# Fused window attention and FFN on one Trainium2 core: from head 12 on, the score products of attention in plain float32 on 64x32 tiles instead of split float32r operands

## Chip, core and metric

The kernel runs on one core of a Trainium2 chip. The metric is device time in microseconds (us), the median of repeated runs. TensorE (PE) does all matrix products. VectorE (DVE), ScalarE (ACT) and GpSimd (POOL) do the elementwise work. SyncE (SP) issues nearly all DMAs.

## The reference

Eight batches of eight heads (64 heads), 512 local and 32 global rows of 64 floats for each head. Every global query sees all 544 keys. A local query sees the 32 global keys and the local keys at most 32 positions away. The rows of all heads then go through a two-layer FFN. Cut to what matters:

```python
k_all = np.concatenate([k_g, k_l], axis=2)
s_g = scale * np.matmul(q_g, k_all.transpose(0, 1, 3, 2))
out_g = np.matmul(sm(s_g), v_all)                 # sm: softmax, sum + 1e-9
s_ll = scale * np.matmul(q_l, k_l.transpose(0, 1, 3, 2))
s_ll = np.where(np.abs(pos[:, None] - pos[None, :]) <= 32, s_ll, -1e9)
s_lg = scale * np.matmul(q_l, k_g.transpose(0, 1, 3, 2))
out_l = np.matmul(sm(np.concatenate([s_lg, s_ll], -1)), np.concatenate([v_g, v_l], 2))
x = concat([out_g, out_l]).transpose(0, 2, 1, 3).reshape(4352, 512)
h = x @ w_in; y = (h - np.tanh(h)) @ w_out        # w_in 512x2048, w_out 2048x512
```

## The kernel before, in words

**FFN.** Each batch's 512 local rows are one chunk, and the 256 global rows are a last one. A chunk has 16 steps. A step is 12 matmuls into the hidden layer (L1062; L1088 for the first chunk's first steps) and 12 out of it (L1125). Operands are float32 numbers split into a rounded high part and a rest, both float32r, and each product is three passes (high x high, high x rest, rest x high). After each step ACT takes tanh (L1070), DVE subtracts (L1073), and the result is split again (L346, L1079).

**Attention, heads 0 to 11** ("plain"). Keys and queries are float32, two heads at a time (a pair) on partitions 0 to 63 and 64 to 127. A float32 product of two plain operands leaves two matmul records in the trace for each matmul in the program. Local scores (L643) are 64-row tiles, 224 columns for each block of 128 queries. Global scores (L553, L554) are 512 and 96 columns for both heads of a pair. Probabilities are transposed by TensorE (L1019) into `turned`, and the products with the values (L695) take both heads side by side, each on 64 columns of the array: 18 + 19 blocks of 32 columns, 1184 columns for each head.

**Attention, heads 12 to 63.** Each head's keys and queries are loaded (L741), transposed by DVE in 32x32 blocks (L745), rounded to a high part and a rest (L346, L754), and moved from partitions to partitions by SP's DMAs, so that high and rest lie on top of each other: keys into `kw` (L843, four DMAs a head), queries within `hi` and `hl` (L848, two a head). Then a head's local scores are eight matmuls of 224 columns with 128 rows (L929 rest, L930 high), and its global scores are two (L878, L879; 384 and 224 columns). DVE takes the maximum (L934, L890), ACT the exponential (L941, L896), POOL the division (L953, L905). Heads 12 to 15 still transpose on TensorE (L1019, two visits of four matmuls a head). From head 16 on (`MOVE`) DVE transposes 32x32 blocks (L997), a DMA writes them to DRAM (`moved`, L1001), and seven DMAs a pair bring them back into `turned` (L675). Global probabilities go over `gt` (L980, then L346).

**What sets the order.** Everything is given to a list scheduler (`Order`) as an operation with an engine, an estimated time, a due time (from the table `CFG`), and the keys it reads and writes. `run()` simulates the engines and writes the instructions in the order of its simulated starts, one fixed order for each engine. On the chip each engine follows its order and waits on semaphores. Attention of a batch is laid between the FFN steps of the batch before. `turned`, the probability buffers and the loaded raw keys and queries have one copy each, and attention uses the PSUM banks 0 to 2.

Of the kernel before, what the change touches and what calls it, by code (L numbers as in the profile page):

```python
# [32 lines left out]
class Later:  # L33


    def __init__(self, pool, shape, tag):
        self.make = lambda: pool.tile(shape, F32R, name=tag, tag=tag)
        self.tile = None
# [167 lines left out]
def kernel(ctx, tc, q_l, k_l, v_l, q_g, k_g, v_g, w_in, w_out, out):  # L206
# [12 lines left out]
    dr = ctx.enter_context(tc.tile_pool(name="dr", bufs=1, space=bass.MemoryType.DRAM))  # L219
# [3 lines left out]
    MOVE = 16  # L223
    PLAIN = 6
    stats_all = cp.tile([P, 4, 16], F32, name="stats")
    stats = [stats_all[:, j] for j in range(4)]
    gt = cp.tile([P, 5, G], F32, name="gt")
# [5 lines left out]
    raw1, kq = rawkq[:, :S], rawkq[:, S:]  # L233
    wraw01 = cp.tile([P, 512, 2], F32, name="wraw01")
    wraw2 = cp.tile([P, 512], F32, name="wraw2")
# [8 lines left out]
    vraw = cp.tile([P, 2, NT, D], F32, name="vraw")  # L244
    joined = [vraw.rearrange("p a t d -> p (a t d)"), wraw2]
# [26 lines left out]
    moved = [dr.tile([P, KC // 32, 2 * NT, 32], F32, name=f"moved{j}") for j in range(2)]  # L272
# [5 lines left out]
    prob = [cp.tile([P, 2 * KC + G], F32, name=f"prob{j}") for j in range(2)]  # L278
# [8 lines left out]
    kw2 = Later(cp, [P, NT, KC], "kw")  # L287
    hi0, hl = Later(cp, [P, S], "hi0"), Later(cp, [P, 2, S], "hl")

    def parts_hi(u):  # L290
        return hl()[:, 0] if u else hi0()

    def part_lo():
        return hl()[:, 1]
# [4 lines left out]
    kgt = Later(cp, [P, H * G], "kgt")  # L299
    qgt = Later(cp, [P, H, 2, G], "qgt")  # L300
# [10 lines left out]
    def bank(shape, j, dt=F32):  # L311
# [6 lines left out]
        elif len(shape) == 4:  # L318
# [4 lines left out]
    CFG = dict(a_g=0.0823, a_gl=20.3051, a_kg=5.3644, a_kq=1.7694, a_ph=9.8391, a_qs=37.5681, a_w=0.3044, a_wn=43.1857, a_xg=33.2801, d_g=63.4309,  # L323
               d_gl=20.8802, d_kg=0.5854, d_kq=14.1069, d_ph=0.45, d_qh=26.732, d_qs=0.6609, d_tg=1.5033, d_tp=30.9704, d_w=35.4231, d_wl=106.2853,
               d_wn=0.9146, d_xg=67.7167, d_y=44.1556, gfirst=0, ho=563.7252, hs=263.6934, lag=-554.6717, last=0.0, newb=2, o_ld=-6186.7772,
               o_pv=-1166.4422, o_pvp=715.1637, o_s=-1347.6614, o_sg=-1415.5434, o_sp=-135.3597, o_t=241.5756, o_tg=456.811, o_tn=-6827.0521,
               o_tpp=-435.6543, o_rd=921.0591, o_vl=-3274.0645, p0=59.5136, pen=45.3181, penp=-188.1742, s_g=44.266, s_gl=16.9975, s_kq=26.1855,
               s_ql=65.9933, s_w=66.4348, s_wl=19.1856, step=539.4635, step1=134.0641, lag0=-705.3437, hs0=198.8445, tol=0.01097, wd0=-392.1115,
               wsp=62.3079, xw=7.7743182, o_ld0=208.6561, o_tn0=444.0832, o_sg0=755.2869, o_tg0=-488.1267, o_s0=-1015.1146, o_sp0=-1339.9745,
               o_t0=786.6386, o_tpp0=12.6795, o_vl0=5.0533, o_vl1=-1566.8932, o_pv0=1125.121, o_pvp0=1054.5986, o_ld1=1734.2237, o_pv1=248.4066,  # L330
               o_pvp1=443.4492, o_s1=-272.1136, o_sg1=-1114.1941, o_sp1=1078.4169, o_t1=339.8555, o_tg1=-620.4031, o_tn1=-475.6504, o_tpp1=659.0213,
               wsp1=13.077, ho0=1146.9578, mw=0.0683195, o_h0=1295.0637, hp=-258.3577, bp0=395.8109, bp1=-328.4325, bp2=-95.9109, bp3=-555.0465,
# [147 lines left out]
    class Pair:  # L480
# [170 lines left out]
        def add_norms(self, p):  # L651
# [11 lines left out]
            for norm, due, st, x in n:  # L663
                add(("P", 0.89), norm, due, r=[st], w=[x])

        def add_fetch(self):
            src = moved[self.j % 2]
            mv = [("mv", self.j % 2, h, p) for h in range(2) for p in range(2)]

# [61 lines left out]

    def add_transposed(name, n, loads, due, u, xfer):

        def load(e, _):
# [659 lines left out]
```

## Time and profile before

| what | value |
|---|---|
| runs, median (lowest to highest) | 975.27 us (974.46 to 976.32) |
| profiled execution, span on the page | 979.0 us (no other time of it is given) |
| TensorE busy, share | 945.6 us, 97% |
| VectorE, ScalarE, GpSimd busy | 601.2, 506.0, 452.1 us |
| granted TensorE clock, mean | 0.992 |
| DMA moved | 129.23 MB; 48.8% of the 16 engines' span for SP's queue |
| last products with the values begin | 828.4 us |

The profiled span is 3.7 us (0.4%) above the median. "Busy" counts an engine while an instruction runs. TensorE's matmuls overlap, so the time one costs is the distance from its start to the next start, not its own length.

### The profile page before, as it was taken

The page shows a single profiled execution, that of the slowest core. Times are in us where ns is not written, and L with a number is a line of the kernel's source. Part 1 is how long each engine was busy: PE and PEld are TensorE (multiplying, and loading weights), DVE is VectorE, ACT ScalarE, POOL GpSimd, SP SyncE. Part 2 cuts the span into 40 slices and gives each one's busy share as a digit, 9 for nine tenths or more (in the row PEclk, how much of TensorE's full clock was granted, in tenths as well). Part 3 has the DMA queues.
Part 4 walks back from the last instruction along what each step waited for, and adds up shares of the span by engine and source line. Part 5 has one row for each costly group of instructions (what it writes and reads, how often), then busy time and mean ns, then how long its engine had stood idle before and what let it go on. Part 6 is the DMA issues. An engine that isn't in the chain of part 4 may idle for free.

```text
span 979.0 us, 17478 instructions
## 1 busy us (share of the span) xinstructions
PE 945.6 (97%) x5246; PEld 774.5 (79%) x5246; DVE 601.2 (61%) x2116; ACT 506.0 (52%) x1381; POOL 452.1 (46%) x560
## 2 busy tenths in 40 slices
PE   7899999999999999999999999999999999999998
PEld 5676787787888788878788778887788788888897
DVE  6876578777747784678738774678738775111110
ACT  5875676755536554555537554565537543222221
POOL 4565767554535453454435553454436442222221
PEclk8999999999999999999999999999999999999999
DMA  8556466577766676677656775677657772100000
GB/s 212 157 137 157 145 174 170 135 162 158 166 137 162 155 161 144 140 162 173 139 113 167 158 167 121 140 163 171 137 114 170 161 179 61 44 1 1 14 31 22
DMA packets 363103, 129.23 MB, mean 132 GB/s; under 512 B 301952, under 2 KB 349952, under 8 KB 363008
## 3 DMA queue, kind: packets, MB, share of 16 engines
q1 hardware_dynamic: 301680, 112.08, 48.8%
q10 hardware_dynamic: 61328, 16.03, 7.1%
q8 instruction: 42, 0.69, 0.3%
q14 instruction: 53, 0.43, 0.2%
HBM read 61.98 MB, written 30.93 MB: 95 GB/s over the span
## 4 chain that ended last, share of the span: by engine, by line
PE 69%; DMA 9%; DVE 7%; ACT 5%; SPq 4%; issue 2%; POOL 2%; ACTq 0%; DVEq 0%; POOLq 0%
PE bank L1125 28%; PE bank L1062 28%; PE bank L695 5%; DMA hl<-hl 3%; PE bank L929 2%; ACT prob L941 2%; SPq L741 2%; PE bank L930 2%; DMA moved<-wraw 1%; POOL prob L953 1%; DVE prob L934 1%; DVE t L1073 1%; DMA out_dram<-wraw 1%; DMA first_q<-in_moe_w_in_dram 1%; SPq L848 1%
## 5 line engine op out<-in xcount | busy, mean ns | idle before, releaser
L1079 POOL TENSOR_TENSOR gates<-t,gates 128x512 fp32r<-128x512 f32 x136 | 176.8, 1300 | 287.0 <-PE bank L1125 181.6
L1125 PE MATMUL bank<-w_out_hi,gates 128*128 128x512 f32 x1088 | 297.0, 393 | 3.1 <-ACT gates L346 2.3
L1125 PEld LDWEIGHTS bank<-w_out_hi,gates 128*128 128x128 f32 x1088 | 202.0, 188 | 47.1 <-ACT gates L346 2.9
L1073 DVE TENSOR_TENSOR t<-bank,t 128x512 f32<-128x512 f32 x136 | 93.5, 688 | 183.9 <-ACT t L1070 182.6
L1070 ACT ACTIVATE t<-bank 128x512 f32<-128x512 f32 x136 | 81.1, 597 | 170.1 <-PE bank L1062 156.8
L1125 PE MATMUL bank<-w_out_lo,gates 128*128 128x512 f32 x544 | 151.9, 393 | 0.1
L1062 PE MATMUL bank<-x_hi,w_in_lo 128*128 128x512 f32 x496 | 134.1, 392 | 0.0
L1062 PE MATMUL bank<-x_hi,w_in_hi 128*128 128x512 f32 x496 | 134.0, 392 | 0.0
L1062 PE MATMUL bank<-x_lo,w_in_hi 128*128 128x512 f32 x496 | 134.0, 392 | 0.0
L953 POOL TENSOR_SCALAR prob<-prob,stats 128x224 f32<-128x224 f32 x240 | 106.8, 460 | 55.0 <-DVE stats L947 15.2
L346 ACT CAST gates<-t 128x512 fp32r<-128x512 f32 x136 | 84.3, 620 | 88.0 <-PE bank L1125 62.6
L941 ACT ACTIVATE prob<-prob,stats 128x224 f32<-128x224 f32 x240 | 112.9, 473 | 30.3 <-DVE stats L934 29.9
L1125 PEld LDWEIGHTS bank<-w_out_lo,gates 128*128 128x128 f32 x544 | 101.1, 189 | 21.9 <-issue 1.1
L1062 PEld LDWEIGHTS bank<-x_hi,w_in_lo 128*128 128x128 f32 x496 | 91.4, 188 | 19.6 <-issue 1.6
L1062 PEld LDWEIGHTS bank<-x_lo,w_in_hi 128*128 128x128 f32 x496 | 91.2, 188 | 19.0 <-issue 1.1
L1062 PEld LDWEIGHTS bank<-x_hi,w_in_hi 128*128 128x128 f32 x496 | 90.2, 188 | 17.5 <-issue 0.5
L934 DVE CUSTOM_DVE_ANT_0 prob<-bank,mask 128x224 f32<-128x224 f32 x240 | 80.8, 385 | 34.1 <-PE bank L930 30.0
L695 PE MATMUL bank<-turned,first_v 128*64 128x160 f32 (+2 forms) x1024 | 72.6, 292 | 2.2 <-DMA turned<-moved 1.5
L695 PEld LDWEIGHTS bank<-turned,first_v 128*64 128x64 f32 (+1 forms) x1024 | 62.0, 136 | 14.3 <-issue 9.9
L980 DVE STREAM_TRANSPOSE gt<-pg 32x160 f32<-32x160 f32 x208 | 67.6, 325 | 3.6 <-POOL pg L905 0.6
L754 POOL TENSOR_TENSOR hl<-rawkq,hl 128x512 fp32r<-128x512 f32 (+1 forms) x30 | 37.0, 1234 | 66.1 <-PE bank L930 36.0
L905 POOL TENSOR_SCALAR pg<-pg,stats 32x608 f32<-32x608 f32 x52 | 39.9, 767 | 57.7 <-DVE stats L902 39.0
(131 smaller groups left out, 1233.7 us busy)
## 6 DMA issues: line engine op xcount, KB each, us to landing
hl<-hl SPq DMA_DIRECT2D x78, 128.0 KB, 2.6
out_dram<-wraw SPq DMA_DIRECT2D x32, 256.0 KB, 3.0
moved<-vraw ACTq DMA_DIRECT2D x36, 224.0 KB, 3.3
first_v<-in_v_l_dram SPq DMA_DIRECT2D x31, 256.0 KB, 3.4
kw<-hl SPq DMA_DIRECT2D x78, 96.0 KB, 2.2
rawkq<-in_k_l_dram SPq DMA_DIRECT2D x104, 64.0 KB, 2.4
rawkq<-in_q_l_dram SPq DMA_DIRECT2D x104, 64.0 KB, 2.5
moved<-wraw ACTq DMA_DIRECT2D x29, 224.0 KB, 3.6
```

What stands on the lines that cost most here:

```text
L346: (nc.scalar.copy if e == "A" else eng[e].tensor_copy)(dst, src)
L695: nc.tensor.matmul(t_[a.e:a.e + D, t % 2, :32 * n], a.v[:k, b, t], a.thi[:k, b, :n, t], start=i == 0, stop=i == 3, skip_group_check=True)
L905: nc.gpsimd.tensor_scalar(pr[:, :608], pr[:, :608], self.st[e0:e0 + 32, 15:16], 1.0, op0=ALU.mult, op1=ALU.mult)
L934: nc.vector.tensor_tensor_reduce(out=self.tile(t)[:, :KC], in0=getattr(self, f"s_{pair}")[:, i, :KC], in1=tile_mask[t], scale=-0.125, scal ...
L941: nc.scalar.activation(x, x, AF.Exp, bias=self.st[:, t:t + 1], scale=-1.0, accum_out=self.st[:, 4 + t:5 + t])
L953: nc.gpsimd.tensor_scalar(x, x, self.st[:, 8 + t:9 + t], 1.0, op0=ALU.mult, op1=ALU.mult)
L980: nc.vector.transpose(gt[r, :c], view(pg[e0:e0 + 32, 32 * q:32 * q + 1], [(P, c), (1, 32)]))
L1062: nc.tensor.matmul(self.h[s][:, j * n:(j + 1) * n], w[:, cc, f * P:(f + 1) * P], self.x()[xi][:, cc, :n], start=part == 0 and cc == 0 and ...
L1070: nc.scalar.activation(tt_[q], self.h[s], AF.Tanh)
L1073: nc.vector.tensor_sub(tt_[q], self.h.pop(s), tt_[q])
L1079: eng[e].tensor_sub(gg[q][1], tt_[q].rearrange("p (k c) -> p k c", k=4), f32(gg[q][0]))
L1125: nc.tensor.matmul(self.acc[tt], g[:, j * nt + tt], low_out(f) if wi else w_out_hi[:, f], start=s == 0 and k == 1, stop=last and k == 3 * ...
```

## The change

From head 12 on, keys and queries stay float32 and unsplit, two heads at a time as in the plain part. The raw rows of a pair are loaded with head 0 on partitions 0 to 63 and head 1 on 64 to 127 (`add_raw`), and one DVE transpose puts the pair's keys into one of two key buffers (`add_keys`) and another its queries into `query` (`add_queries`). A block of 128 queries is cut into four of 32. Each multiplies only the 128 columns it can see (32 global keys and three blocks of 32 local keys), as a 64-row, 32-column tile: 4 blocks x 4 x 2 heads = 32 matmuls a pair (`add_band_scores`). Global scores are computed for two pairs at once (`Quad`), each pair on 64 columns of the array. Probabilities are transposed by DVE as 32x32 squares (`sq`), and 16 DMAs a pair move them directly into `turned` (`add_squares`), without DRAM. Global probabilities are transposed by DVE directly into `turned` (`add_global_turn`). The split, the partition moves by DMA, the way over DRAM, and the transposes on TensorE of heads 12 to 15 are gone. The table `CFG` has new numbers throughout.

```diff
+    SQ = 4 * G
+    sq = cp.tile([P, 4, 2, NT, G], F32, name="sq")
-    moved = [dr.tile([P, KC // 32, 2 * NT, 32], F32, name=f"moved{j}") for j in range(2)]
...
-    kw2 = Later(cp, [P, NT, KC], "kw")
-    hi0, hl = Later(cp, [P, S], "hi0"), Later(cp, [P, 2, S], "hl")
+    NB = 29
+    keys = [Later(cp, [P, NB * G], t, F32) for t in ("kw", "hl")]
+    query = Later(cp, [P, S], "hi0", F32)
...
-               o_sp2=376.7277, o_t2=479.2751, o_tg2=146.273, o_tn2=-406.5557, o_tpp2=-362.6754, o_vl2=-234.6789, o_m=-1681.6994, o_mpp=3490.5823)
+               o_g2=-1787.1182, o_tg2=21682.7815, o_sq2=1060.2028, o_vl2=11176.8598, o_pv2=-590.8468, o_pvp2=0)
...
+        def add_raw(self):
+            def load(a, src):
+                def fn(e, _):
+                    for two in range(2):
+                        x = src[self.b, 2 * self.jj + two].rearrange("(b s) d -> s b d", s=32)
+                        for half in range(2):
+                            p0 = 64 * two + 32 * half
+                            eng[e].dma_start(raws_kq[a][p0:p0 + 32].rearrange("s (b d) -> s b d", d=32),
+                                             x[:, :, 32 * half:32 * half + 32])
...
+            def turn(e, _):
+                nc.vector.transpose(kw()[:, 64:64 + 768].rearrange("p (g c) -> p g c", c=96)[:, :, :64],
+                                    raws_kq[0].rearrange("p (g c) -> p g c", c=64))
...
+                    for t in tiles:
+                        for c in range(4):
+                            n = NT * t + c - 1
+                            at = G * (2 + 3 * (n // 2) + n % 2 if n >= 0 else 0)
+                            for a in self.heads:
+                                r = slice(a.e, a.e + D)
+                                nc.tensor.matmul(box["s"][a.two][G * c:G * c + G, t], query()[r, t * P + G * c:t * P + G * c + G],
+                                                 kw()[r, at:at + SQ], start=True, stop=True)
...
+                    for n in range(4):
+                        k = 6 if n == 1 + c % 2 else c + n - (n > 1 + c % 2)
+                        eng[e].dma_start(turned[32 * (k % 4):32 * (k % 4) + 32, k // 4, c].rearrange("p t c -> p (t c)"),
+                                         sq[32 * c:32 * c + 32, n].rearrange("p a t c -> p (a t c)"))
...
+                    for g in range(4):
+                        r = slice(32 * g, 32 * g + 32)
+                        nc.vector.transpose(turned[r, 0, 4, NT * a.two:NT * a.two + NT], view(pg[p0:p0 + 32, 32 * g:32 * g + 1], [(P, NT), (1, G)]))
...
+                for x in self.pairs:
+                    r = slice(64 * x.u, 64 * x.u + 64)
+                    q = gqs()[:, 0, x.jj].rearrange("p h g -> p (h g)")
+                    k = keys[x.u]()
+                    parts.append([(s0[r], q, view(k[:, :1], [(96, 8), (64, 2), (1, G)])), (s1[r], q, view(k[:, :1], [(64, 3), (1, G)], 24 * G))])
...
-                    nc.tensor.matmul(t_[:, i, :KC], part_lo()[:, q], kw2()[:, t], start=True, stop=False)
-                    nc.tensor.matmul(t_[:, i, :KC], parts_hi(self.hl)[:, q], kw2()[:, t], start=False, stop=True)
```

TensorE's order in the middle of the program, before: the products of one pair end, the FFN goes on (`bank_101`, `bank_102` and up), and one head's global and local scores stand between its matmuls.

```order
L695 MATMUL bank_99<-turned,first_v 64x160 x2
L1125 MATMUL bank_105<-w_out_lo,gates 128x512
...
L878 MATMUL bank_98<-kw,qgt 128x384
L879 MATMUL bank_100<-kw,qgt 128x224
L1062 MATMUL bank_101<-x_hi_79,w_in_hi 128x512 x4
...
L929 MATMUL bank_99<-kw,hl 128x224
L930 MATMUL bank_99<-kw,hi_1220 128x224
...
L1125 MATMUL bank_105<-w_out_hi,gates 128x512
```

The same place now: the scores of a whole pair stand in one piece (`kw` or `hl` is the key buffer, `hi` the queries, `bank_92` and `bank_94` the two heads; the 32 rows alternate between the heads), and one group of global scores serves four heads.

```order
L1126 MATMUL bank_96<-w_out_hi,gates 128x512
L709 MATMUL bank_92<-hl,hi_1175 32x128
L709 MATMUL bank_94<-hl,hi_1175 32x128
...
L1063 MATMUL bank_95<-x_hi_75,w_in_hi 128x512 x4
...
L879 MATMUL bank_93<-kw,qgt 64x512
L879 MATMUL bank_93<-hl,qgt 64x512
L879 MATMUL bank_92<-kw,qgt 64x96
L879 MATMUL bank_92<-hl,qgt 64x96
```

A pair had two visits of eight score matmuls and two of global scores. It now has one visit of 32 small matmuls and half a visit of four.

SP's order before, for a head and the fetch of a pair: partition moves of keys (L843) and queries (L848) stand between the loads, and the fetch from DRAM (L675) behind them.

```order
L843 DMA kw<-hl 64x2x192
L843 DMA kw<-hl 64x2x160
...
L741 DMA rawkq<-in_k_l_dram 32x16x32 x2
L741 DMA rawkq<-in_q_l_dram 32x16x32 x2
L848 DMA hl<-hl 64x512 x2
L675 DMA turned<-moved_88 32x256
L675 DMA turned<-moved_88 32x2x256
L675 DMA turned<-moved_88 32x3x256 x2
```

SP's order now, for two pairs: loads of raw keys and queries run ahead by pairs, and each pair's 16 square moves stand in one piece.

```order
L665 DMA rawkq<-in_k_l_dram 32x16x32 x8
L725 DMA turned<-sq 32x256 x16
L606 DMA first_v<-in_v_l_dram 128x8x64
L606 DMA first_v<-in_v_l_dram 64x8x64
L618 DMA first_v<-in_v_g_dram 32x4x64 x2
L665 DMA rawkq<-in_q_l_dram 32x16x32 x8
L725 DMA turned<-sq 32x256 x16
```

A load that follows the squares waits on SP until the squares have been issued, and the values (`first_v`) of the next pair stand behind the squares of this one. No DMA is left on the way from the raw load to the scores.

## Rows read from the trace of the kernel before

**Rows 1.** Table by stretch: us, busy time by engine, granted clock, DMA share, GB/s.

```profile
220.00:832.00 612.00, 599.08 (x3336) 493.06 (x3335) 422.33 (x1541) 320.21 (x918) 284.67 (x363) 1.00 0.66 149
832.00:979.00 147.00, 142.66 (x720) 121.65 (x718) 18.15 (x28) 37.18 (x64) 35.10 (x28) 0.99 0.05 19
```

**Rows 2.** Waits of TensorE over the span: us in total, times, longest.

```profile
PE bank L929 <- DMA hl<-hl: 8.5, 11, 1.4
...
PE bank L695 <- DMA turned<-moved: 1.5, 2, 1.1
...
PE bank L878 <- DVE wraw L997: 1.1, 1, 1.1
```

**Rows 3.** Timeline of TensorE, local scores of a head: start, us, engine, line.

```profile
510.47 1.07 PE L1062 MATMUL bank<-x_hi,w_in_hi 128*128 128x512 f32 x4
511.38 0.26 PE L929 MATMUL bank<-kw,hl 128*128 128x224 f32 x1
...
512.26 1.09 PE L1062 MATMUL bank<-x_lo,w_in_hi 128*128 128x512 f32 x4
513.19 0.39 PE L1062 MATMUL bank<-x_hi,w_in_lo 128*128 128x512 f32 x1
```

**Rows 4.** Timeline of TensorE, global scores of a head.

```profile
517.73 0.34 PE L878 MATMUL bank<-kw,qgt 128*128 128x384 f32 x1
...
518.00 1.09 PE L1062 MATMUL bank<-x_lo,w_in_hi 128*128 128x512 f32 x4
518.93 0.40 PE L1062 MATMUL bank<-x_hi,w_in_lo 128*128 128x512 f32 x1
```

**Rows 5.** Timeline of TensorE, products of a pair with the values.

```profile
500.50 1.07 PE L1062 MATMUL bank<-x_lo,w_in_hi 128*128 128x512 f32 x4
501.50 2.24 PE L695 MATMUL bank<-turned,first_v 128*64 128x160 f32 x32
503.67 1.20 PE L1062 MATMUL bank<-x_hi,w_in_lo 128*128 128x512 f32 x4
504.71 0.62 PE L1125 MATMUL bank<-w_out_hi,gates 128*128 128x512 f32 x2
```

**Rows 6.** Timeline of TensorE, plain float32 global scores of a pair (heads 0 to 11).

```profile
82.75 0.61 PE L1062 MATMUL bank<-x_hi,w_in_lo 128*128 128x512 f32 x2
83.30 1.07 PE L553 MATMUL bank<-first_kw,first_m 128*64 128x512 f32 x2
...
84.46 0.51 PE L1088 MATMUL bank<-x_hi,w_in_hi 128*128 128x512 f32 x1
84.81 0.40 PE L1088 MATMUL bank<-x_lo,w_in_hi 128*128 128x512 f32 x1
```

**Rows 7.** Timeline of TensorE, plain float32 local scores, half a pair.

```profile
109.73 1.03 PE L643 MATMUL bank<-first_kw,first_q 64*128 64x224 f32 x8
110.69 1.20 PE L1062 MATMUL bank<-x_hi,w_in_hi 128*128 128x512 f32 x4
```

**Rows 8.** Timeline of TensorE, one visit of transposes (heads 12 to 15).

```profile
163.90 0.60 PE L1019 MATMUL bank<-idr,prob 128*128 128x128 f32 x4
164.26 1.18 PE L1125 MATMUL bank<-w_out_hi,gates 128*128 128x512 f32 x4
```

**Rows 9.** Weight loads as a visit of products begins, first one, then two.

```profile
657.26 0.13 PEld L695 LDWEIGHTS bank<-turned,first_v 128*64 128x64 f32 x1 [0.35 <-DVE kw L346]
657.26 0.14 PEld L695 LDWEIGHTS bank<-turned,first_v 128*64 128x64 f32 x2 [0.35 <-DVE kw L346]
```

**Rows 10.** The same inside this visit, just after a wait.

```profile
658.34 0.13 PEld L695 LDWEIGHTS bank<-turned,first_v 96*64 96x64 f32 x1 [0.61 <-issue]
658.34 0.17 PEld L695 LDWEIGHTS bank<-turned,first_v 96*64 96x64 f32 x2 [0.61 <-issue]
```

**Rows 11.** SP's fetches of squares: ns min/median/max, first and last start; landing.

```profile
L675 SPq DMA_DIRECT2D turned<-moved x168: 302/427/1966, 218.0 to 822.9; - x168
...
DMA to landing us min/median/max: 1.7/2.3/4.3
```

More of the change, by code (lines that the diff above doesn't have):

```diff
@@ L339 @@
+    PHASE = [{k[:-1]: v for k, v in CFG.items() if k.startswith("o_") and k.endswith(x)} for x in "012"]
     order = Order({"att": (0, 1, 2), "h": (0, 1, 2, 3), "acc": (4, 5, 6, 7), None: tuple(range(8))})
@@ new lines, in add_queries, with turn, add_band_scores, mm @@
+        def add_queries(self):
+            def turn(e, _):
+                nc.vector.transpose(query(), raws_kq[1])
+            add(("D", 0.69), turn, self.due(self.C["o_qt"]), r=["kq"], w=["hk0"])
+        def add_band_scores(self, *ranges):
+            kw, u = keys[self.u], self.u
+            s = [(f"s{a.two}", a.i) for a in self.heads]
+            box = {}
+            def mm(tiles):
+                def fn(e, tags):
+                    if "s" not in box:
+                        box["s"] = [bank([P, NT, SQ], tags[x]) for x in s]
+                        for a in self.heads:
+                            a.scores = box["s"][a.two]
+                    for t in tiles:
+                        for c in range(4):
+                            n = NT * t + c - 1
+                            at = G * (2 + 3 * (n // 2) + n % 2 if n >= 0 else 0)
+                            for a in self.heads:
+                                r = slice(a.e, a.e + D)
+                                nc.tensor.matmul(box["s"][a.two][G * c:G * c + G, t], query()[r, t * P + G * c:t * P + G * c + G],
+                                                 kw()[r, at:at + SQ], start=True, stop=True)
+                return fn
+            for j, tiles in enumerate(ranges):
+                add(("T", 0.215 * len(tiles)), mm(tiles), self.due(self.C["o_l"] + self.C["o_lp"] * j), r=[f"kw{u}", f"kg{u}", "hk0"], w=s,
+                    res=["p00", "p10"],
+                    alloc=[(x, "att") for x in s] if j == 0 else (), rows=0.8, tail=0.05, mode=1)
+            for a in self.heads:
+                a.add_band()
@@ new lines, in add_global_turn, with turn @@
+        def add_global_turn(self):
+            for a in self.heads:
+                def turn(e, _, a=a):
+                    p0 = 64 * self.u + 32 * a.two
+                    for g in range(4):
+                        r = slice(32 * g, 32 * g + 32)
+                        nc.vector.transpose(turned[r, 0, 4, NT * a.two:NT * a.two + NT], view(pg[p0:p0 + 32, 32 * g:32 * g + 1], [(P, NT), (1, G)]))
+                        if g < 3:
+                            nc.vector.transpose(turned[r, 1, 4, NT * a.two + NT - 1], pg[p0:p0 + 32, 512 + 32 * g:544 + 32 * g])
+                add(("D", 1.75), turn, self.due(self.C["o_tg"]), r=["pg0"], w=[f"hg{a.two}"])
@@ L778, in keys, with turn @@
             return fn
[L780 removed]
+        def turn(a):
             def fn(e, _):
[L782 to L788 removed]
@@ L789, in add_globals @@
-        add(("S", 0.6), keys(lo, slice(D, P)), due, r=["lk"], w=["kgtl"], res=["gl0"], xfer=0.4)
-        add(("S", 1.2), queries(lo, 1), due, r=["lq"], w=["qgtl"], res=[("wraw", 3, 0), ("wraw", 3, 1)], xfer=0.8)
+                x = gqs()[:, 1, :, a]
+                if a == 0:
+                    nc.vector.transpose(kgt(), x)
+                else:
+                    for two in range(2):
+                        r = slice(64 * two, 64 * two + 64)
+                        nc.vector.transpose(gqs()[r, 0, :, two], x[r])
```

405 lines of the change are left out of this document (173 added, 232 removed).

## The prediction

> **What bounds the kernel now.** The table by stretch comes first. Between 220 and 832 us, where heads 12 to 63 are worked on beside the FFN, TensorE is busy 599 of 612 us at the full clock (granted 1.00, which is 2.4 GHz), while DVE is busy 422 us, ACT 320 and POOL 285 [rows 1]. From 832 us on only FFN matmuls are left, 147 us. So the end is set by how much TensorE has to do, plus the 13 us of its idling in that stretch. Work on DVE, ACT, POOL and SP counts only through waits. The list of TensorE's waits is the second view: the largest of the span is for the query move `hl<-hl`, 8.5 us in 11 waits, and 1.5 us are for the squares fetched from DRAM and 1.1 us for a bank or buffer that a DVE transpose held [rows 2]. The third view is TensorE's timeline, read from start to start, because its matmuls overlap. Four FFN matmuls take 0.91 us (510.47 to 511.38), 0.23 us each [rows 3]. Whatever lies between FFN matmuls beyond that is the price of a visit.
>
> **What is removed on TensorE.** A head's local scores run from 511.38 to 512.26, 0.88 us, and the four FFN matmuls behind them take 0.93 instead of 0.91: 0.90 us [rows 3]. A head's global scores run from 517.73 to 518.00, again with 0.02 us behind them: 0.29 us [rows 4]. Together 1.19 us a head, 4.76 us for four heads. A visit of transposes is 0.36 us, and its four FFN matmuls behind it last 1.18 us instead of 1.07 [rows 8, 5]: 0.47 us, eight times (heads 12 to 15), 3.8 us.
>
> **What is added on TensorE.** No row shows 64x32 tiles. I price a visit of plain float32 work from two visits that the trace has.
> - Products: 501.50 to 503.67 is 2.17 us, the four FFN matmuls ahead take 1.00 instead of 0.91, and those behind 1.04: 2.17 + 0.09 + 0.13 = 2.39 us, for 1184 columns in each of two heads side by side [rows 5].
> - Plain global scores: 83.30 to 84.46 is 1.16 us, 0.10 more ahead (0.55 for two FFN matmuls) and 0.12 more behind (0.35 for one): 1.38 us for 608 columns [rows 6].
>
> The difference, 1.01 us for 576 columns, is 1.75 ns a column, and 0.32 us is left as the fixed price of entering and leaving. A check with the plain local scores, 448 columns in each of two row tiles: 0.78 + 0.32 = 1.10 by this rule, and 0.96 measured plus 0.09 ahead (as for the products) and 0.13 behind (1.20 instead of 1.07) is 1.18 [rows 7, 5]. So row tiles may cost 0.08 more.
>
> A pair's band scores are 32 matmuls of 128 columns. If all eight tiles (two row halves by four column quarters) run side by side, that is four rounds, 512 columns: 0.90 + 0.32 = 1.22, or 1.30 with the 0.08. I take 1.28, near the row that also tiles rows. The scores for four heads are the 608 columns of the plain visit, two column halves side by side: 1.38. So four heads cost 2 x 1.28 + 1.38 = 3.94 instead of 4.76 us, 0.82 less. Times 13 (52 heads) this is 10.7 us.
>
> The bounds of the band visit: below, 1.22. Above, two readings. First, the issue of matmuls. The second head's weight load starts 0.01 us after the first (two end at 0.14, one at 0.13) where the queue had filled while the FFN ran [rows 9]. Just after a wait, with the queue empty, it starts 0.04 us later [rows 10], which I read as the pace at which the sequencer hands on matmuls. 32 x 0.04 = 1.28, plus 0.38 (0.32 with most of the 0.08), is 1.66 us. Should the 0.04 hold for each of the two records of a matmul, it is 2.56 + 0.38 = 2.94. Second, the trace never shows more than two tiles that read the same partitions. If four cannot stream at once, rounds take twice the time: 1.80 + 0.38 = 2.18. I keep 1.28, because a visit follows 12 or more FFN matmuls in which the queue fills, and because two column tiles run at no loss [rows 5].
>
> Loads on two tiles 0.01 us apart [rows 9] are 64 x 0.01 = 0.64 us for all records of a band visit, less than the 0.90 us of streaming; so I let streaming set the price. The Trainium skill ("TensorE: Matmul & The Clock Gate", Part 1, on the gap of 56 ns) says otherwise: matmuls never start closer together than about 25 ns, however few their columns. By that figure an estimate for 64 records is 1.6 us, a visit of 1.98, and the sum would be 18 us worse. Part 3 of the same page gives about 4 ns between matmuls on different tiles, with which the 0.01 us agrees [rows 9]. No run here shows eight tiles.
>
> **Waits removed.** The queries no longer take a DMA between their transpose and the scores, so the 8.5 us for `hl<-hl` go. The 1.5 us for fetches and the 1.1 us for the buffer go with the way over DRAM: 11.1 us [rows 2].
>
> **Waits added.** Squares: 16 issues a pair at 0.43 us and a landing of 2.3 us are 9.2 us from the first issue to the last landing [rows 11], against seven issues (5.3 us) before. `turned` has one copy, so the squares of a pair start only when the products before it are done. In the new order at least 72 FFN matmuls and a band visit lie between two products, 72 x 0.23 + 1.3 = 17.9 us, which hides 9.2. Without that cover a pair would pay 9 us. Queued behind the squares on SP are the next pair's values and raw loads; they are needed a pair (two dozen us) later, and SP has fewer issues than before. The global scores of four heads stand 12 FFN matmuls (2.7 us) behind a band visit in most batches and take a PSUM bank that DVE must empty first, and TensorE's in-order queue would hold the FFN behind them. Late next would be the exponentials, eight in a row on ACT, ahead of a tanh that TensorE needs. I cannot price these from rows. Below nothing is excluded by the fixed order: a wait only adds. I put 5 us, about half of what went, with 0 and 20 us (0.8 us a pair) as ends. DVE, ACT and POOL lose work (no split, 128 instead of 224 columns a block) and were under 70% busy [rows 1]: nothing. The first 200 us are re-ordered by the new table; their work is the same, and I give them plus or minus 4 us.
>
> **The sum.** 979.0 - 10.7 - 3.8 - 11.1 + 5 = 958.4 us of span. The median of the runs is 3.7 us below the profiled span, a factor of 0.9962: 954.7, **955 us**, 2.1% less.
>
> **The rivals.**
> - *Four column tiles do not stream at once.* Band visit 2.18, 0.90 more, times 26: 23.4 us, 981.8 of span, 978 us. Slower than before. It decides from a visit of 2.07 us on, where the 20.6 us of the sum are used up. For it: every plain visit in the trace has at most two tiles. Against it: two are free of loss [rows 5].
> - *The sequencer's pace.* Visit 1.66, 0.38 more, 9.9 us: 968.3, 965 us. For it: the 0.04 us [rows 10], and a visit is twice as many matmuls as one of products. With the pace for each record, 2.94: 43 us more, 998 us. Against that: the 0.01 us [rows 9].
> - *A floor under the starts of all tiles together*, for each record half way between the 0.01 and the 0.04 us, 0.025 [rows 9, 10]: 64 records take 1.6 us, a visit 1.98, 0.70 more, 18.2 us: 976.6 of span, 973 us. The rule of the Trainium skill's page above (Part 1) is such a floor; the 0.01 us speaks against it [rows 9].
> - *New waits eat it.* 0.8 us a pair for banks, squares or a late tanh: 20 us instead of 5, 973.4 of span, 970 us; with a bad start, 975.
> - *Nothing new waits*: 953.4 less 2 from the start, 948 us; it is inside the forecast's range.
>
> **How the numbers follow.** Forecast (948 to 962) 0.60; sequencer's pace 0.12; new waits 0.10; four tiles not at once 0.10; the floor 0.05; pace for each record 0.03. 0.2% of 975 is 2 us, about what a measurement here can tell from no change. Faster: 0.60 + 0.12 + 0.06 of the new waits = 0.78. Same (973.3 to 977.2): half of the floor's case and some of the new waits, 0.07. Slower: 0.15, the four tiles, the pace for each record, and the ends of the others. From 946 to 977 lie the forecast, the pace, the new waits and the floor, some 0.82.
>
> **What would show it.** A band visit of 1.2 to 1.35 us beyond the FFN's own pace, from the last FFN start ahead to the second behind; weight loads some 0.01 us apart in it. A visit of global scores near 1.4 us. No wait of TensorE for a DMA of queries. Few waits for `turned<-sq`. TensorE's waits between 220 us and the last products around 5 us. The last products near 809 us instead of 828. Wrong it would be if band visits pass 2 us, or if waits for PSUM banks or squares sum to more than 15 us.

## The result, and the profile after

The changed kernel takes 950.45 us (median of 4 runs, 948.05 to 950.55), the kernel before 975.8 us on the same chip (4 runs, 974.46 to 977.72): a ratio of 0.974, 95% interval 0.972 to 0.976, or 25 us less. In the changed kernel's line numbers the band scores of a pair are L709, the global scores of a quad L879, the products L758, the transfers of squares L725, the global transposes of heads 0 to 11 L585.

The table by stretch of the changed kernel, whose profiled span is 946.3 us, answers to [rows 1]:

```profile
0.00:220.00 220.00, 201.74 (x1453) 154.87 (x1454) 147.65 (x523) 132.96 (x373) 119.59 (x186) 0.98 0.59 144
220.00:809.00 589.00, 589.00 (x4335) 470.80 (x4334) 293.99 (x1153) 215.66 (x647) 186.75 (x277) 1.00 0.30 66
```

TensorE does not idle between 220 and 809 us, where before it idled 13 us of 612. DVE, ACT and POOL all do less, and the DMA share falls from 0.66 to 0.30. The list of TensorE's waits, which answers to [rows 2], has no transfer of queries or squares left in it; its longest wait, 5.2 us for the global probabilities of heads 0 to 11, lies ahead of the stage that was changed (before, the waits at that place were 2.3 us in all):

```profile
PE bank L585 <- POOL pg L564: 7.2, 3, 5.2
PE bank L512 <- DMA first_raw<-in_k_l_dram: 2.9, 1, 2.9
PE bank L1020 <- POOL prob L964: 2.6, 5, 1.4
```

The timeline of TensorE shows a band visit and, after 12 FFN matmuls, a quad's visit; they answer to [rows 3, 4]:

```profile
292.90 0.39 PE L1126 MATMUL bank<-w_out_hi,gates 128*128 128x512 f32 x1
293.22 1.16 PE L709 MATMUL bank<-hl,hi 64*32 64x128 f32 x64
294.31 1.19 PE L1063 MATMUL bank<-x_hi,w_in_hi 128*128 128x512 f32 x4
295.33 0.84 PE L1063 MATMUL bank<-x_lo,w_in_hi 128*128 128x512 f32 x3
...
296.24 1.07 PE L1063 MATMUL bank<-x_hi,w_in_lo 128*128 128x512 f32 x4
297.24 0.64 PE L879 MATMUL bank<-kw,qgt 128*64 128x512 f32 x1
...
298.41 1.21 PE L1063 MATMUL bank<-x_hi,w_in_hi 128*128 128x512 f32 x4
299.46 0.85 PE L1063 MATMUL bank<-x_lo,w_in_hi 128*128 128x512 f32 x3
```

Read from start to start, as in the prediction: the band visit is 293.22 to 294.31, 1.09 us; its first start comes 0.32 us after the FFN matmul ahead of it instead of 0.23, and the four FFN matmuls behind take 1.02 instead of 0.91: 1.09 + 0.09 + 0.11 = 1.29 us. The quad's visit is 1.17 + 0.09 (1.00 for the four ahead) + 0.14 = 1.40 us. In the raw records 25 of the 26 band visits cost 1.29 us (the first is longer) and the 13 quads 1.40 to 1.41. The weight loads of that band visit, 64 of them, are one row:

```profile
293.22 0.89 PEld L709 LDWEIGHTS bank<-hl,hi 64*32 64x32 f32 x64 [0.35 <-issue]
```

### The profile page after: what moved, and what is told of

It reads as the page before. It is cut to its first block, busy times and chain, and to the rows that moved or that the text cites. A ratio compares the mean times of both kernels' runs of the same rounds, so it can differ in the third digit from the quotient of the medians.

```text
span 946.3 us, 18378 instructions
## 1 busy us (share of the span) xinstructions
PE 923.7 (98%) x6462; PEld 739.3 (78%) x6462; DVE 465.9 (49%) x1707; ACT 378.8 (40%) x1068; POOL 340.2 (36%) x491
## 4 chain that ended last, share of the span: by engine, by line
PE 89%; DMA 3%; ACT 3%; DVE 3%; issue 1%; POOL 1%; ACTq 0%; DVEq 0%; POOLq 0%; SPq 0%
PE bank L1126 39%; PE bank L1063 38%; PE bank L758 6%; PE bank L709 3%; PE bank L879 2%; DMA wraw<-in_moe_w_in_dram 1%; DMA first_q<-in_moe_w_out_dram 1%; DVE sq L412 1%; ACT prob L958 1%; DMA wraw<-in_moe_w_out_dram 1%; ACT turned L338 0%; DMA first_raw<-in_k_l_dram 0%; PE bank L1020 0%; PE bank L545 0%; ACT w_out_hi L338 0%
## 5 line engine op out<-in xcount | busy, mean ns | idle before, releaser
L1126 PE MATMUL bank<-w_out_hi,gates 128*128 128x512 f32 x1088 | 287.5, 394 | 1.5 <-ACT gates L338 1.1
L993 POOL TENSOR_SCALAR prob<-prob,stats 128x128 f32<-128x128 f32 x208 | 74.9, 381 | 60.5 <-DVE stats L989 55.5
L984 ACT ACTIVATE prob<-prob,stats 128x128 f32<-128x128 f32 x208 | 80.6, 389 | 28.5 <-DVE stats L979 27.9
L758 PE MATMUL bank<-turned,first_v 128*64 128x160 f32 (+2 forms) x1024 | 72.8, 294 | 0.1
L758 PEld LDWEIGHTS bank<-turned,first_v 128*64 128x64 f32 (+1 forms) x1024 | 63.0, 137 | 11.7 <-issue 9.9
L739 DVE STREAM_TRANSPOSE turned<-pg 32x128 f32<-32x128 f32 x208 | 62.6, 301 | 4.3 <-POOL pg L899 1.0
L979 DVE CUSTOM_DVE_ANT_0 prob<-bank,mask 128x128 f32<-128x128 f32 x208 | 45.9, 287 | 14.9 <-PE bank L709 14.9
L775 DVE TENSOR_TENSOR x_lo<-bank,x_hi 128x256 fp32r<-128x256 f32 x64 | 26.8, 419 | 38.1 <-ACT x_hi L338 38.1
L996 DVE STREAM_TRANSPOSE sq<-prob 128x512 f32<-128x512 f32 x52 | 36.3, 704 | 14.0 <-DMA turned<-sq 4.7
```

The lines of the kernel that those rows point to most:

```text
L739: nc.vector.transpose(turned[r, 0, 4, NT * a.two:NT * a.two + NT], view(pg[p0:p0 + 32, 32 * g:32 * g + 1], [(P, NT), (1, G)]))
L758: nc.tensor.matmul(t_[a.e:a.e + D, t % 2, :32 * n], a.v[:k, b, t], a.thi[:k, b, :n, t], start=i == 0, stop=i == 3, skip_group_check=True)
L979: nc.vector.tensor_tensor_reduce(out=x[:, t], in0=self.scores[:, t], in1=bands[0 if t == 0 else 2 if t == NT - 1 else 1](), scale=-0.125, ...
L984: nc.scalar.activation(x[:, t], x[:, t], AF.Exp, bias=self.st[:, t:t + 1], scale=-1.0, accum_out=self.st[:, 4 + t:5 + t])
L993: nc.gpsimd.tensor_scalar(x[:, t], x[:, t], self.st[:, 8 + t:9 + t], 1.0, op0=ALU.mult, op1=ALU.mult)
L996: nc.vector.transpose(sq[:, :, self.two].rearrange("p n t c -> p t n c"), x.rearrange("p t (n c) -> p t n c", c=G))
```

## The experiments

**Theory.** The gain has two parts: cheaper visits (the prices of the prediction's sum), and the end of the waits that the moves between transpose and scores made. **Rival A:** the visits are cheap only in the order in which the multiplies are written, or not at all, and the gain is one of waits alone. **Rival B:** the late starts (a late start is the time by which a matmul begins later than at the usual distance behind the one ahead of it) went because the new table of numbers makes a better order, not because the moves went.

### The order of multiplies within a visit: tiles_in_turn, heads_in_turn, quads_apart

The first swaps the two loops of the band visit:

```
-                    for t in tiles:
-                        for c in range(4):
+                    for c in range(4):
+                        for t in tiles:
```

> The changed kernel with the score multiplies of a band visit in another order: column tile 0 of both query tiles first, then column tile 1, and so on, so that consecutive multiplies meet only two of the eight tiles (the two heads' rows). Theory 1, TensorE starts its multiplies strictly in program order and one that finds its tile taken holds up all behind it: 64 records, two at once, 109 ns apart, are 3.5 us, the visit costs 3.5 + 0.4 = 3.9 us where the changed kernel's costs 1.29, and 26 visits add 68 us: ratio to the kernel before about 1.04. Theory 2, each tile is fed from a queue of its own, so that the order within a visit is of no account: no change, ratio 0.974. A queue a few multiplies deep would lie between (visit about 2 us, ratio 0.99).

The second moves the loop over the pair's heads outermost within a call:

```
-                    for t in tiles:
-                        for c in range(4):
...
-                            for a in self.heads:
+                    for a in self.heads:
+                        for t in tiles:
+                            for c in range(4):
```

> The changed kernel with the multiplies of one head of a pair first and the other's after them, so that consecutive multiplies meet four tiles. Theory 1 (strict order): 64 records, four at once, 109 ns apart, are 1.74 us, the visit costs 2.16 us, 26 visits add 0.87 each, 23 us: ratio 0.997. Theory 2 (a queue for each tile): no change, ratio 0.974.

The third takes the quad's multiplies pair by pair:

```
-                for two in zip(*parts):
+                for two in parts:
```

> The changed kernel with the two pairs of a quad's global scores not alternated: both multiplies of the one pair, then both of the other. Theory 1 (strict order): the second multiply of the first pair waits 0.85 us for the first, and the other pair behind it, so the quad's visit costs 1.38 + 0.85 = 2.2 us, and 13 visits add 11 us: ratio 0.985. Theory 2 (a queue for each tile): no change, ratio 0.974.

Measured: 958.34 us, ratio 0.982 (0.979 to 0.984); 956.57 us, 0.981 (0.978 to 0.983); 950.38 us, 0.974 (0.972 to 0.976). Timeline of TensorE around one band visit, first of tiles_in_turn, then of heads_in_turn:

```profile
222.54 1.07 PE L1126 MATMUL bank<-w_out_hi,gates 128*128 128x512 f32 x4
223.54 1.44 PE L709 MATMUL bank<-kw,hi 64*32 64x128 f32 x64
224.91 1.20 PE L1126 MATMUL bank<-w_out_hi,gates 128*128 128x512 f32 x4
```

```profile
222.73 0.84 PE L1126 MATMUL bank<-w_out_hi,gates 128*128 128x512 f32 x3
223.50 1.38 PE L709 MATMUL bank<-kw,hi 64*32 64x128 f32 x64
224.81 1.20 PE L1126 MATMUL bank<-w_out_hi,gates 128*128 128x512 f32 x4
```

From its first start to the first FFN start behind it the visit takes 1.37 and 1.31 us where the changed kernel's takes 1.09. So 0.28 and 0.22 us a visit, times 26: 7.3 and 5.7 us, against 7.9 and 6.1 us between the medians. For the band both theories miss: strict order would have cost 68 and 23 us, a queue for each tile nothing. The third case, a queue a few multiplies deep, is right in kind, but it put the visit at 2 us, where with the 0.09 ahead and some 0.13 behind it costs about 1.6. So records must run ahead of one that finds its tile taken, but not without limit: the visit takes 1.09 us when the order goes round all eight tiles, and 0.2 to 0.3 us more when it dwells on two or four. For the two pairs of a quad, with four multiplies in all, the order is of no account. Rival A falls: even in the worse orders a visit stays near its predicted price. Eight tiles stream at once: by the 109 ns of the expectation 64 records are 0.87 us on eight tiles and 1.74 on four, and the visit took 1.09.

### The fixed price of a visit: two_visits

```
-               o_l2=-2676.9949, o_lp2=-272.8582,
+               o_l2=-2676.9949, o_lp2=10000.0,
```

> The changed kernel with the second half of the band's multiplies due much later, so that in 8 of the 26 pairs the planner cuts the visit into two of 16 multiplies each. If a visit has a fixed price of 0.32 to 0.42 us beside its records (the price law of the prediction), a half visit costs 0.44 + 0.4 = 0.85 us, the two together 1.7 instead of 1.29, and the kernel is 8 x 0.4 = 3.3 us longer if nothing else moves (ratio 0.977). If there is no fixed price (rival: the 0.4 is an artefact of the first and last record of a visit of this size), half visits cost 0.65 and the time stays at 0.974.

Measured: 1262.51 us, ratio 1.295 (1.292 to 1.297). As a measurement of time it failed: the late half shifted later placements, and TensorE waited, as its list of waits shows:

```profile
PE bank L709 <- DVE hi L688: 64.6, 17, 5.0
PE bank L758 <- DMA first_v<-in_v_g_dram: 53.5, 5, 12.0
PE bank L758 <- DMA turned<-sq: 50.3, 19, 8.5
```

But eight visits were cut, as expected, and of the 16 halves all but the first take 0.60 us to the next start. Those among FFN matmuls give the price:

```profile
219.92 1.07 PE L1063 MATMUL bank<-x_lo,w_in_hi 128*128 128x512 f32 x4
220.92 0.67 PE L709 MATMUL bank<-hl,hi 64*32 64x128 f32 x32
221.52 1.19 PE L1063 MATMUL bank<-x_hi,w_in_lo 128*128 128x512 f32 x4
222.54 0.84 PE L1126 MATMUL bank<-w_out_hi,gates 128*128 128x512 f32 x3
```

0.60 + 0.09 (1.00 ahead) + 0.11 (1.02 behind) = 0.80 us for half the records, where the whole costs 1.29. Two halves cost 1.60, so the fixed price of a visit is 0.31 us; the prediction had 0.32 from other shapes. That leaves 0.98 us for the columns, where the prediction's price a column gives 0.90.

### The cover of the squares: squares_halved

```
-                        eng[e].dma_start(turned[32 * (k % 4):32 * (k % 4) + 32, ...
+                        for r in (0, 16):
+                            eng[e].dma_start(turned[32 * (k % 4) + r:32 * (k % 4) + r + 16, ...
```

> The changed kernel with each of a pair's 16 transfers of squares cut into two of 16 partitions, so 32 issues on SyncE; the planner's costs are left alone, so the order of the work is the same. In the changed kernel an issue takes 0.59 us, not 0.43, a pair's 16 take 10.1 to 12.2 us, and the products begin 7.0 to 17.8 us after the last of them (a landing of 1.8 us lies in that). Theory 1, the transfers cost nothing only because of that room: 16 more issues of 0.59 us are 9.4 us, which the seven pairs with 7.0 to 7.7 us of room and the two early ones with 0.9 and 3.0 do not have; at 9.4 + 1.8 - 7.3 = 3.9 us each for the seven and some 17 us for the early two TensorE waits about 45 us, ratio 1.02, and most of its wait is for these transfers. Theory 2, an issue costs by the bytes it moves: half as many bytes take half as long and nothing changes, ratio 0.974. Theory 3: late products push the later ones back, so that only the first wait is paid: plus 10 us, ratio 0.984.

Measured: 1124.19 us, ratio 1.152 (1.148 to 1.157), far worse than any of the three. The row of the squares' transfers in the changed kernel (ns min/median/max of an issue, first and last start), and the same row here:

```profile
L725 SPq DMA_DIRECT2D turned<-sq x416: 512/589/1738, 133.4 to 786.6; - x139
...
DMA to landing us min/median/max: 1.8/1.9/4.0
```

```profile
L726 SPq DMA_DIRECT2D turned<-sq x832: 512/587/1804, 132.7 to 968.0; - x167
...
  DVE sq L997: 221.7, 24
  PE bank L759: 16.8, 4
```

An issue of 16 partitions takes the same 0.59 us as one of 32, so theory 2 falls: 32 of them are 19 us. Who waited is the lesson: TensorE itself only 16.8 us in four waits for squares (and 32.5 us for the values, which stand behind the squares on SyncE), but VectorE 221.7 us in 24, for `sq` to be read before it may write the next pair's squares. TensorE's own list then names VectorE (`turned` at L740, the global part, 52.4 us in 22 waits), which is behind that wait in VectorE's queue. There is one copy of `sq` and one of `turned`, and the chain of transposes, 32 issues (21 us from the first to the end of the last), landing and products closes on itself: by the raw records the first issues of the pairs come 32.4 us apart on the average, 23 times from 203.0 to 948.3 us. No later pair gets room back, so theory 3 falls too; theory 1 had the mechanism and counted it too low, since it let each pair start from the old room. In the table by stretch TensorE idles 76 us, and the granted clock falls too, to 0.92 on the average where the changed kernel has 1.00:

```profile
220.00:809.00 589.00, 513.35 (x3557) 406.50 (x3556) 232.62 (x930) 172.26 (x522) 150.37 (x225) 0.92 0.26 56
```

### The moves alone: before_moves_once, before_moves_empty, before_moves_aside

All three edit the kernel before. The first takes the moves out of the plan:

```
+            if self.i == 2 * PLAIN:
                 add(("S", 1.2), keys(hi, slice(0, D)), due, r=[hk], w=["kw0"], xfer=0.9)
                 add(("S", 1.2), keys(lo, slice(D, P)), due + 0.5, r=["lk"], w=["kl0"], xfer=0.9)
-            add(("S", 0.6), queries(hi), due + 0.5, r=[hq], w=[hk], xfer=0.6)
-            add(("S", 0.6), queries(lo), due + 0.5, r=["lq"], w=["lk"], xfer=0.6)
```

> The kernel before without its direct transfers of keys to windows and of queries from one half of the partitions to the other, except for the first head of the stage (left out: the scores of all later heads read that head's keys, and queries of the wrong parts). Everything else is as before. Theory 1: those moves, between the transposes and the scores, make TensorE's late starts in the kernel before, which I count in the raw records as 22 us after 120 us; without them some 15 of the 22 go, ratio 0.985. Theory 2: the late starts come from the many operations that VectorE, ScalarE and GpSimd do for the split into two parts, which stay: ratio 1.00 (0.997 to 1.003). With fewer transfers the planner may also place work differently, which the trace would show in the order of TensorE's work.

Measured: 977.34 us, ratio 1.000 (0.999 to 1.002). By itself this would speak for theory 2. Its TensorE no longer waits for a query, but its order differs from that of before in many places, as the expectation had allowed for: late starts between FFN matmuls rose (my count from the raw records: 1.8 us before, 8.7 here) while those entering local scores fell (12.5 to 2.1). So the next keeps the plan and empties the steps:

```
                 def fn(e, _):
-                    nc.sync.dma_start(f32(x()[:D]), f32(x()[D:]))
+                    if self.i == 2 * PLAIN:
+                        nc.sync.dma_start(f32(x()[:D]), f32(x()[D:]))
```

and likewise for the keys.

> The kernel before with the same order of work on every computing engine, in which the planned moves of keys to windows and of queries between the partitions' halves issue nothing after the first head of the stage (left out: later heads' scores read that head's keys, and queries of the wrong parts). Unlike the run that took the moves from the planner too, nothing else is placed anew. Theory 1: those transfers make most of the 22 us of late starts in the kernel before, 12.5 us of it entering the local scores: minus 10 to 18 us, ratio 0.982 to 0.990. Theory 2: they are only the last of several things that are late, and the work of the split on VectorE and ScalarE would be late next: minus 0 to 4 us, ratio 0.996 to 1.00.

Measured: 960.35 us, ratio 0.985 (0.983 to 0.987), 15 us less than before; the two traces have the same order of work on every computing engine. Theory 1 holds. Its table by stretch answers to [rows 1]:

```profile
220.00:809.00 589.00, 588.95 (x3315) 491.64 (x3313) 417.04 (x1528) 317.42 (x914) 284.43 (x361) 1.00 0.48 107
```

TensorE's idling is gone with nothing changed but the moves; VectorE, ScalarE and GpSimd are as busy as before. Late starts after 120 us fall, by the same count, from 24 us (the expectation had counted 22) to 5, and those entering local scores from 12.5 to 0.1. This takes rival B away for these 15 us: neither the new table nor the lighter work of the other engines is needed for them. The third asks whether the moves hurt by their traffic, by sending it elsewhere:

```
-                    nc.sync.dma_start(f32(x()[:D]), f32(x()[D:]))
+                    nc.sync.dma_start(f32(x()[:D]) if self.i == 2 * PLAIN else aside2, f32(x()[D:]))
```

> The kernel before with the same order of work on every computing engine, in which the moves of keys and queries are issued as before, as many and as large, but go, after the first head of the stage, to a place in DRAM that nobody reads (left out: as in the run that leaves them empty, later heads' scores read old keys and queries of the wrong parts). It tells apart why leaving them out gave 15 us. Theory 1, the scores and the work behind them wait for a chain of transpose, move, landing: then the traffic alone costs nothing and the time is that of the empty moves, ratio 0.985 (960 us). Theory 2, the moves' issues on SyncE and their packets delay the other transfers (raw loads, values, squares): then the time stays near the kernel before, ratio 0.995 to 1.00. In between it would be both, in shares that the ratio gives.

Measured: 1025.83 us, ratio 1.052 (1.049 to 1.054): neither theory. The edit made a wait of its own. All query moves now write one place, and 43 times one waits on SyncE for the landing of the last; the waits of SyncE's queue:

```profile
SPq L850 <- DMA aside<-hl: 42.7, 23, 2.4
...
SPq L850 <- DMA aside<-hi: 37.2, 20, 2.5
```

and TensorE waits, 23.8 us in 12 waits, for squares queued behind them:

```profile
PE bank L697 <- DMA turned<-moved: 23.8, 12, 5.0
```

So the question is not answered. What the run does show is that a SyncE queue that stands 80 us for the query moves came with 50 us more time, though the planner's order was the same. In the kernel before the same queue stands 44 us for the local scores to be done with the one window buffer, with all later transfers behind it; this wait is gone where the moves go aside, so the two runs differ by more than the place that the moves write:

```profile
SPq L843 <- PE bank L930: 44.0, 26, 3.1
```

### One move put back: query_moved

```
-                nc.vector.transpose(query(), raws_kq[1])
+                nc.vector.transpose(query()[:D], raws_kq[1][:D])
...
+            def move(e, _):
+                nc.sync.dma_start(query()[D:], query()[:D])
...
+            add(("S", 0.6), move, self.due(self.C["o_qt"]) + 0.5, r=["kq"], w=["hk0"], xfer=0.6)
```

> The changed kernel with one transfer put back between the transpose of the queries and the scores: VectorE transposes the first head's queries, and SyncE's queue copies them to the second head's partitions (left out: the second head's own queries). The planner counts it with the 0.6 us that it had in the kernel before. Theory 1 (such moves made the late starts of before): a move takes 0.6 us of issue and about 1.8 us until it lands, and each of the 26 band visits starts late by part of that, 0.2 to 0.8 us: plus 5 to 20 us, ratio 0.98 to 0.995, and TensorE waits for the moved query. Theory 2: with one query buffer and the queries transposed well ahead of the scores, one move in a pair is hidden: ratio 0.974 (0.971 to 0.977).

Measured: 954.10 us, ratio 0.977 (0.974 to 0.980), 3.6 us above the changed kernel. The intervals of the ratios overlap, but none of its four runs is as short as any of the changed kernel's. The largest of TensorE's waits is again L585; for the move there is one, of 0.2 us:

```profile
PE bank L585 <- POOL pg L564: 6.8, 3, 5.0
...
PE bank L762 <- DMA turned<-sq: 1.2, 1, 1.2
...
PE bank L713 <- DMA hi<-hi: 0.2, 1, 0.2
```

No band visit begins late, by the raw records, but two of the 26 stand inside, between the first head's first records and the second head's, which need the moved query: the visit at 442.5 us takes 1.69 instead of 1.09 us, and here the profile names the move; the one at 203.5 us takes 1.51. In the other 24 the move is hidden. After 400 FFN matmuls the run is 3.8 us behind the changed kernel (191.9 against 188.1 us), ahead of most of the heads in question. So theory 2 in the main: one move in a pair cost about 1 us, and most of the difference is a new order at the start. What made the moves of the kernel before worse is not shown by this run: their number (312 issues, six a head, against one a pair), the one buffer that the keys are moved into, or a shorter lead.

### The table: old_table, weights_late26, weights_late34

old_table puts the kernel before's numbers into the changed kernel's table wherever both have a name:

```
-    CFG = dict(a_g=-12448.4861, a_kg=-240156.236, a_ph=1.1877, ...
+    CFG = dict(a_g=0.0823, a_kg=5.3644, a_ph=9.8391, ...
```

> The changed kernel with the numbers of the planner's table as the kernel before had them, for the 76 names that both tables have; the ten new names keep theirs. Theory 1, the gain is in the new structure (cheaper visits, fewer transposes, no moves) and not in the order: the time stays within 0.5% of the changed kernel's, ratio 0.97 to 0.98. Theory 2, what the removed late starts gave (some 20 us) came from the order that the new numbers make: ratio 0.99 to 1.0, with TensorE waits beyond 220 us where the changed kernel has none. A much longer time would say that the old numbers do not fit the new steps at all.

Measured: 1257.21 us, ratio 1.288 (1.284 to 1.292), the third case of the expectation. TensorE waits for squares and for transposed queries; that the old due times put the new steps too close to each other is my reading of it, not shown:

```profile
PE bank L748 <- DMA turned<-sq: 128.6, 38, 12.3
PE bank L699 <- DVE hi L678: 99.0, 17, 9.9
```

So the structure does not keep its gain under every order; it needs one fitted to it. The last two try to better the changed kernel. Its wait for L585 comes about like this, in its timeline (SyncE, ScalarE, GpSimd, TensorE; in brackets the idle time ahead and what ended it):

```profile
110.22 0.42 SPq L392 DMA_DIRECT2D wraw<-in_moe_w_in_dram  x1
...
114.97 0.66 ACT L403 ACTIVATE wraw<-wraw 128x512 f32<-128x512 f32 x1 [5.00 <-DMA wraw<-in_moe_w_in_dram]
...
117.75 4.03 POOL L993 TENSOR_SCALAR prob<-prob,stats 128x128 f32<-128x128 f32 x8 [3.42 <-DVE stats L989]
...
123.10 0.77 POOL L564 TENSOR_SCALAR pg<-pg,stats 64x608 f32<-64x608 f32 x1
...
123.93 0.79 PE L585 MATMUL bank<-idr,pg 64*128 64x64 f32 x5 [5.19 <-POOL pg L564]
```

A load of FFN weights lands 4.7 us after its issue; ScalarE's queue stands 5.0 us for it, its eight exponentials follow late, then GpSimd's eight scalings, then, behind a split of FFN weights, the one TensorE needs. Right behind this wait the granted clock is 0.50, which is 1.2 GHz, with TensorE busy all the time; the table by stretch:

```profile
124.00:128.00 4.00, 4.00 (x21) 2.90 (x23) 3.01 (x7) 1.99 (x8) 2.46 (x2) 0.50 0.29 83
```

The edit tells the planner of a later landing, here the first of two values:

```
-                w=keys if WIDE else [wj], xfer=1.46 if n else 2.2)
+                w=keys if WIDE else [wj], xfer=2.6)
```

> The changed kernel with the planner told that a load of FFN weights takes 2.6 us instead of 1.46 until it lands (in the changed kernel such a load lands 3.8 to 4.7 us after its issue, ScalarE's queue stands 5.0 us behind one at 110 to 115 us, and TensorE's one long wait of 5.2 us for the last plain pair's global probabilities follows from that). Theory: the planner puts that rebias later, the wait goes, minus 3 to 5 us, ratio 0.969. Rival: every placement moves with it and the gain is lost in an order that the table's numbers were not fitted to: the same or some per cent slower, as in the two runs whose planner's numbers were changed.

> As the last, with 3.4 us. Theory: the wait goes, ratio 0.969; rival: an order that fits worse, the same or slower.

Measured: 969.54 us, ratio 0.995 (0.992 to 0.997), and 975.78 us, 1.000 (0.999 to 1.002). The rival holds. From the first one's table by stretch and its list of waits:

```profile
0.00:220.00 220.00, 187.19 (x1288) 139.69 (x1289) 141.51 (x487) 130.89 (x367) 118.07 (x183) 0.95 0.57 138
220.00:809.00 589.00, 589.00 (x4393) 470.58 (x4392) 299.69 (x1173) 216.29 (x647) 186.75 (x278) 1.00 0.31 68
```

```profile
PE bank L585 <- POOL pg L564: 8.4, 2, 7.5
PE bank L758 <- DMA turned<-sq: 8.0, 2, 7.7
```

The stage of heads 12 to 63 is again without idling; the loss is in the first 220 us, where TensorE is busy 187 us instead of 202. The wait for L585 did not go with the first value; with the second it fell to 2.5 us, but the run as a whole was longer still. No version here beats the changed kernel.

## Why the prediction was right, point by point

- **Prices.** Band visit 1.28 predicted, 1.29 measured; quad 1.38 and 1.40. Four heads cost 2 x 1.29 + 1.40 = 3.98 instead of 4.76, 0.78 less, 10.1 us in 13 quads against the predicted 10.7. The law of a fixed price and a price per column, taken from products and plain global scores, held for a shape that the trace had never shown, together with the 0.06 us that was put on top of its 1.22 for row tiles. That addition was a choice near one row; two_visits confirmed the fixed part and puts the addition on the columns. The rivals that raised the visit's price (four column tiles not at once, the sequencer's pace, a floor under all starts) needed 1.66 us or more.
- **The floor under starts.** The 64 loads of a band visit took 0.89 us, 0.014 us each with the pauses for occupied tiles. Its 64 matmul records start within the same 0.89 us, the first eight 6 to 7 ns apart in the raw records. The 25 ns of the Trainium skill ("TensorE: Matmul & The Clock Gate", Part 1, on the gap of 56 ns) would have made 1.6 us of the 64; no such floor shows across eight tiles, and the trace sides with the 4 ns of Part 3 of that page in kind, if not in size.
- **Waits removed.** This term was mis-sized: 11.1 predicted from [rows 2], 15.1 measured as the difference of medians when the moves alone were emptied (975.4 to 960.35 us), 21 us in the profiled spans (979.0 to 957.7). The other two waits of the term, for squares and for the buffer, are gone from the list of that run too. The list of waits shows only TensorE's idle time. A start that is late by less than the rest of the matmul ahead leaves none, and one inside a visit less than it costs (0.2 us for 0.6 in query_moved): entering local scores the raw records have 12.5 us of lateness, the list 8.5. How the 15 us divide between late landings and SyncE's blocked queue stays open, since before_moves_aside brought a wait of its own.
- **Waits added.** 5 predicted for banks, squares and a late tanh in the stage; none came there. The one that came, 5.2 us for L585 with half the clock behind it, lies in the stretch that the prediction gave plus or minus 4 us.
- **Squares.** They are hidden, as predicted, though the sum of 9.2 us was too small: issues take 0.59, not 0.43 us, and landing 1.9, not 2.3. A pair's 16 take 10.1 to 12.2 us of issue, some 12 to 14 us with the landing. From 203 us on the products began 7.0 to 17.8 us after the last issue. With 9.4 us more the kernel lost 174 us; where between the two the loss begins was not measured.
- **The sum.** In medians: 15.1 for the moves, 10.1 for the prices and 3.8 for the transposes [rows 8] make 29.0 us; 25.4 was measured. The profiled executions put the difference of 3.6 us ahead of the stage. After 400 FFN matmuls the changed kernel stands at 188.1 us and the one with emptied moves at 185.6. By the prices, and with the scores and transposes that each has done by then, the changed kernel should be 2.1 us ahead there. So by this estimate it loses some 4.6 us in the stretch that holds L585's wait and the half clock; how much of it is theirs was not shown. The predicted 955 is 4.5 us too high, 4.0 of it by the first of these terms. The last products began at 799.4 us and not near 809: this sign missed. The factor 0.9962 was a wrong reading as well: a run's time is as a rule about 1.8 us above its span (948.05 for 946.3), so the profiled execution of before, at 979.0, was probably slower than any of its runs, which went from 971.3 to 979.8. The forecast does not hang on it: 20.6 us off the median of 975.27 is 954.7 as well.

## What to carry to other kernels

Here a visit of small tiled multiplies cost a fixed 0.3 us and then its columns divided by the tiles that stream at once, provided the order went round all tiles; two shapes in the trace priced a third to within 0.07 us. Look for a DMA between two steps of an in-order chain not only in the list of waits but in late starts, and test it by emptying the step while the plan stays as it is: taking it out of the plan as well hid 15 us behind a new order. A transfer that is hidden has a margin; count its issues at the price of their own queue, and ask what waits to overwrite its source.

## What was not expected of the hardware

- The tile order cost only 0.2 to 0.3 us a visit, where a strict order would have cost 2.6 and 0.9: so records for free tiles must start while earlier ones for occupied tiles still wait, up to some depth that was not measured.
- An issue of 16 partitions took as long on SyncE's queue as one of 32: 0.587 and 0.589 us.
- The kernel before scatters by 8.5 us over 17 runs (971.3 to 979.8 us); with its moves emptied, 4 runs lie within 1.5 us, but 4 are few.
